# Exponents taken head by head out of PSUM, and batch 1 handled like the later batches

## Chip, cores and metric

One core of a Trainium2 chip runs one program. The metric is the device time of one execution in microseconds, the median of several runs. The core has five engines, named here as in the profile: PE (TensorE), DVE (VectorE), ACT (ScalarE), POOL (GpSimd) and SP (SyncE, which issues all DMAs).

## What is computed

Attention with pooled keys and values (batch 8, 8 heads, 576 queries, head size 64, 72 pooled keys), and a SwiGLU layer on its result (4608 tokens, 512 to 1536 to 512), all in float32 accuracy.

```python
k_p = k.reshape(B, H, Sp, pool, D).mean(axis=3)      # pool = 8, Sp = 72
v_p = v.reshape(B, H, Sp, pool, D).mean(axis=3)
scores = scale * np.matmul(q, k_p.transpose(0, 1, 3, 2))
attn = np.exp(scores - np.max(scores, axis=-1, keepdims=True))
attn = attn / (np.sum(attn, axis=-1, keepdims=True) + 1e-09)
x = np.matmul(attn, v_p)   # then tokens x 512
g = x @ w_gate
out = (g * (1.0 / (1.0 + np.exp(-g))) * (x @ w_val)) @ w_out
```

## The kernel before

The 4608 tokens are cut into nine tiles of 512. Each tile is put together from attention pieces of up to 128 queries of one batch: 40 pieces in all, four in tile 0, five in tile 1 (its first of 64 queries ends batch 0, the other four are of batch 1); the last piece of batch 1 is the first of tile 2. Accurate products are made of halves: an operand is cut into a high and a low float16 part (for the last layer, into an fp32r and a bfloat16 part), and three products replace one.

For each tile and each of 12 chunks of the hidden layer a step makes gate and value products. A plain step (L773 to L777) does 24 products of 512 columns; a fast step (L858, L925) uses Strassen's scheme, with 42 products of 256 columns and some copies by ACT (L937, L939, L946) and additions by DVE (L942, L947) between them. Tiles 0 and 1 are plain. Chunks of weights are loaded and decoded in the first part (L992, `chunk`): shift, sign, join on DVE, ACT and POOL, a sum of sizes over all rows by PE (L303, L304) into one of two attention banks of PSUM, a scale, then high halves by ACT (L384) and low halves by DVE (L389). Later each chunk is converted for fast steps (L789) on DVE, POOL and ACT, and each tile's x is prepared for them (L824). The output layer runs at the end from L1432 on and the change does not touch it.

A piece is asked for (`ask`, L1233) and answered (`answer`, L1243). PE makes scores into two banks, one for even and one for odd heads (L578). DVE takes the maxima of each half out of PSUM (L587) and writes the difference to SBUF (L588), upon which the bank is given back. ACT takes the exponential of all 576 elements in one instruction (L595, L599), DVE sums them by head (L605, L616) and inverts the sums. The batches differ in the rest. `SPLIT = 2` calls batches 0 and 1 old. For an old batch the keys are summed in groups of eight by DVE or POOL (L405 to L407), and the values by PE with a matrix of ones on the diagonal (L501); the weights are normalised (on DVE, or on POOL, L625), cut into halves by ACT and POOL (L638 to L645), turned by a transposing DMA and multiplied with the values so that x comes out turned (L663 to L666), from where ACT and DVE cut it into halves (L689, L693). For a later batch the host has laid out keys and values as six parts, which POOL adds (L1153, `kv_part`, L1169 to L1171) into a place called box, of which there are two by turns; weights are not normalised, the products come out with queries on rows (L673 to L679), DVE divides (L683), ACT and POOL cut into halves (L1332, L1333), and a second transposing DMA turns x (L1337).

The order of all instructions on all engines is made by a planner in the kernel (`Order`, L64): each line of work is a generator that gives, step by step, engine, assumed time and conditions; at each turn the engine with the earliest ready work takes, among the operations that are ready about then, that of the best rank. Banks and buffers are pools that are got and put back (L761). Every engine then works through its queue in that order, and a waiting instruction holds up all behind it.

Of the kernel before, what the change touches and what calls it, by code (L numbers as in the profile page):

```python
# [17 lines left out]
P = 128  # L18
# [6 lines left out]
SPLIT = 2  # L25
# [21 lines left out]
BANKS = "val", "val"  # L47
VALUES = 0.9
LENT = "gate"
PIECE_RANK = 0, 0.5, 1.2, 1.3, 2.2, 2.8, 3.4, 4, 4.6  # L50
# [141 lines left out]
def attention_then_swiglu(  # L192
# [57 lines left out]
    for i in range(4):  # L250
# [16 lines left out]
    logunit = const.tile([P, 1], F32, name="logunit")  # L267
    nc.gpsimd.memset(logunit, LOGUNIT)

    spare = early.tile([P, 2 * NJ * SP + 6 * NJ * P // 2], F32, name="spare", tag="early")  # L270
    ksum = [
        spare[:, i * NJ * SP : (i + 1) * NJ * SP].rearrange("p (j s) -> p j s", j=NJ)
        for i in range(2)
    ]
    vst = spare[:, 2 * NJ * SP :].bitcast(F16).rearrange("p (i j f) -> p i j f", i=6, j=NJ)
    p2s = const.tile([P, B, 4], F32, name="p2s")
    inv = const.tile([P, B, 3], F32, name="inv")
    vst_h, vst_l, vst_f = ([vst[:, 2 * n + i] for i in range(2)] for n in range(3))
# [14 lines left out]
    def fields():  # L293
        for i in range(2):
            nc.gpsimd.memset(halves[i][:, 2 * NJ * P : OLD], 0.0)
            nc.gpsimd.memset(vst_h[i], 0.0)
            nc.gpsimd.memset(vst_l[i], 0.0)
# [138 lines left out]
    KV = H * D + D + NJ * SP  # L436
    TAIL = 2 * SP - P

    def box(b):

        i = b % 2
        if i not in home:
            whole = raw.tile([P, 12 * P * 2], F32, name="box", tag="raw")
# [20 lines left out]
    def move_k(b):  # L464
        nc.scalar.copy(box(b)["k"].rearrange("p j n -> p (j n)"), home["ks", b % 2])

    def move_left(b):
        left = home["left", b % 2]
        nc.scalar.activation(left, left, AF.Copy, scale=inv[:, b, 2:3])

    def spread_left(b):
        left = home["left", b % 2].unsqueeze(1).broadcast_to([P, H, D])
        nc.gpsimd.tensor_mul(box(b)["vm"], left, masks.unsqueeze(2).broadcast_to([P, H, D]))

    def split_v(b, part):
        src, sv = home["vs", b % 2][:, : H * D], inv[:, b, 2:3]
# [104 lines left out]
    def less_max(b, n, pss, sc=None, groups=(0, 1)):  # L581
        sc = sc or buffer(at, [P, H, SP], F32, "sc")
        mx = small.tile([P, 2, GH], F32, name="mx")
        heads = "p (j g) s -> p g j s"
        for g in groups:
            pv = pss[g][:n, : GH * SP].rearrange("p (h s) -> p h s", h=GH)
            nc.vector.tensor_reduce(out=mx[:n, g], in_=pv, axis=AX.X, op=ALU.max)  # L587
            nc.vector.tensor_tensor(  # L588
                out=sc[:n].rearrange(heads, g=2)[:, g], in0=pv,
                in1=mx[:n, g].unsqueeze(2).broadcast_to([n, GH, SP]), op=ALU.subtract,  # L590
            )
        return sc

    def exponentials(n, sc):
        nc.scalar.activation(sc[:n], sc[:n], AF.Exp, scale=EXPSCALE)  # L595

    def weights(b, n, sc):

        nc.scalar.activation(  # L599
            sc[:n], sc[:n], AF.Exp, bias=logunit[:n], scale=EXPSCALE  # L600
        )

    def row_sums(n, sc):
        sm = small.tile([P, H], F32, name="sm")
        nc.vector.tensor_reduce(out=sm[:n], in_=sc[:n], axis=AX.X, op=ALU.add)  # L605
        return sm

    def one_over(n, sm):
        ri = small.tile([P, H], F32, name="ri", bufs=4)
        nc.vector.tensor_scalar_add(sm[:n], sm[:n], 1e-9 * UNIT)  # L610
        nc.vector.reciprocal(ri[:n], sm[:n])
        return ri

    def inverse_sums(n, sc):
        sm = small.tile([P, H], F32, name="sm")
        nc.vector.tensor_reduce(out=sm[:n], in_=sc[:n], axis=AX.X, op=ALU.add)  # L616
        nc.vector.tensor_scalar(
            out=sm[:n], in0=sm[:n], scalar1=1e-9, scalar2=1.0 / UNIT, op0=ALU.add, op1=ALU.mult
        )
        ri = small.tile([P, H], F32, name="ri", bufs=4)  # L620
# [79 lines left out]
    def scales(bs, mt):  # L700
# [10 lines left out]
        for old in (True, False):  # L711
# [5 lines left out]
            if old:  # L717
                nc.vector.tensor_single_scalar(r, r, 1.0 / UNIT, ALU.mult)
# [26 lines left out]

    ahead = [(i, *sub) for i in range(len(tiles)) for sub in tiles[i][2]]
# [10 lines left out]
    def f_room(name):  # L757
# [8 lines left out]
            "x": [(xp, "x1"), (const, "wo0")], "mid": [0, 1, 2], "qt": [0, 1], "xt": [0, 1], "half": [0, 1],  # L766
# [225 lines left out]
    def chunk(c):  # L992
# [23 lines left out]
        if len([w for w in spent if w[0] is raw]) == RAW_USES + 2 and where[0] is raw:  # L1016
            order.done("boxes", t)
# [78 lines left out]
    def pooled_values(b):  # L1096
# [3 lines left out]
        for g in (2, 0, 1):  # L1100
            order.start(("early", (VALUES, SECOND + 0.3)[b] + 0.01 * g), values_in(b, g, where, max(t, tb)))
# [11 lines left out]
        order.start(("early", (VALUES + 0.02, SECOND + 0.32)[b]), left_values(b, t))  # L1113
# [3 lines left out]
        put(BANKS[b], where, max(t, tl[0]))  # L1117
# [36 lines left out]
    def kv_part(b, c, ready):  # L1154
        n, t0 = yield get("mid")
        _, t1 = yield get("load")
# [8 lines left out]
        dst = home["kv", b % 2][:, cs]  # L1165
# [11 lines left out]
    def prep(b):  # L1177

        split = yield flag("boxes")
        if b > SPLIT + 1:  # L1180
            split = yield flag(("split", b - 2))
        box(0)
        box(1)
        t = 0
        for c in range(6):
            order.start(("kv", b + 0.1 * c), kv_part(b, c, split))
# [3 lines left out]
        t = yield op("DVE", 750, lambda: largest(mx, home["vs", b % 2]), t)  # L1190
# [11 lines left out]
        if b - 2 >= SPLIT:  # L1202
# [40 lines left out]
    def answer(t):  # L1243
# [19 lines left out]
        put("qt", t["qt"], tp)  # L1263
        for g in range(2):
# [538 lines left out]
```

## Time and profile before

| | |
|---|---|
| median of 3 runs | 963.73 us (963.48 to 965.11) |
| the profiled execution | 958.7 us |
| its span in the trace | 956.9 us |
| PE busy | 895.9 us (94%) |
| DVE busy | 717.6 us (75%) |
| POOL busy | 580.4 us (61%) |
| ACT busy | 468.9 us (49%) |
| DMA, mean | 153 GB/s |

The page gives busy times of each engine over the span of one execution. A busy PE is not a PE at its peak, since matmuls are pipelined and their ends are modelled. Durations of instructions that follow each other on an engine can overlap, so the distance of two starts is often less than the first one's duration. Where an engine is idle the trace names what ended the wait.

### The profile page before, as it was taken

The numbers are of one execution on the slowest core, as the hardware profiler recorded it, in microseconds if no ns is written. First come the engines' busy times: TensorE is split into PE (matmuls) and PEld (weight loads), VectorE is DVE, ScalarE is ACT, GpSimd is POOL, SyncE is SP. The second block draws the span as 40 slices with busy tenths as digits, with TensorE's granted clock in tenths as the row PEclk, the third lists the DMA queues.
The fourth block names the chain that finished last, engine by engine and source line by source line (L and its number), as shares of the span: only waits on it lengthen the run. The fifth ranks groups of instructions, "written<-read, shape, count | busy, mean of one in ns | idle before, by whom it ended". The sixth has DMA issues, their size and how long they took to land. (4 is left out here: it accounts for less than half of the span.)

```text
span 956.9 us, 17399 instructions
## 1 busy us (share of the span) xinstructions
PE 895.9 (94%) x6636; PEld 629.2 (66%) x6658; DVE 717.6 (75%) x1087; ACT 468.9 (49%) x809; POOL 580.4 (61%) x502
## 2 busy tenths in 40 slices
PE   5788898998989889999999999999899899999998
PEld 5775354444656667888888888888655455555554
DVE  7889898698877798688877645467737769496781
ACT  5578553334245455566664544355624344444442
POOL 3534998989988898454523404022646578678692
PEclk9799899999999999999999999999999999999999
DMA  9947857848748556557572421135560440806301
GB/s 342 289 123 245 264 149 188 227 117 210 187 127 220 171 116 165 151 116 173 136 161 81 97 72 57 56 108 196 195 217 23 164 188 21 309 23 241 111 23 66
DMA packets 134419, 146.53 MB, mean 153 GB/s; under 512 B 81600, under 2 KB 102080, under 8 KB 132032
## 3 DMA queue, kind: packets, MB, share of 16 engines
q1 hardware_dynamic: 134336, 145.42, 51.7%
q8 instruction: 52, 0.85, 0.4%
q14 instruction: 31, 0.25, 0.1%
HBM read 86.51 MB, written 40.89 MB: 133 GB/s over the span
## 5 line engine op out<-in xcount | busy, mean ns | idle before, releaser
L1600 PE MATMUL ps<-low,wsh 128*128 128x512 bf16 x384 | 146.2, 381 | 5.7 <-DVE low L1487 4.1
L879 PEld LDWEIGHTS <-mixed 128*128 128x128 f16 x1332 | 129.2, 98 | 23.4 <-issue 5.6
L879 PEld LDWEIGHTS <-wgv_h 128*128 128x128 f16 x1184 | 114.3, 98 | 33.2 <-issue 15.1
L723 ACT ACTIVATE hf<-ps,un 128x512 f32<-128x512 f32 (+1 forms) x112 | 74.8, 669 | 102.7 <-PE ps L879 62.3
L879 PE MATMUL ps<-xc,mixed 128*128 128x256 f16 x888 | 118.2, 274 | 3.5 <-ACT ps L939 3.5
L726 DVE SCALAR_TENSOR_TENSOR hf<-hf,ps 128x512 f32<-128x512 f32 (+1 forms) x112 | 74.1, 663 | 57.4 <-ACT hf L723 57.0
L879 PE MATMUL ps<-xc,wgv_h 128*128 128x256 f16 x592 | 104.8, 273 | 9.3 <-DVE ps L947 7.7
L777 PE MATMUL ps<-x,wgv_l 128*128 128x512 f16 (+1 forms) x304 | 110.5, 364 | 2.6 <-DVE wgv_l L389 2.6
L775 PE MATMUL ps<-x,wgv_h 128*128 128x512 f16 (+1 forms) x304 | 110.7, 364 | 0.4 <-ACT wgv_h L384 0.4
L776 PE MATMUL ps<-x,wgv_h 128*128 128x512 f16 (+1 forms) x304 | 110.6, 364 | 0.0
L731 DVE SCALAR_TENSOR_TENSOR hf<-ps,un,hf 128x512 f32<-128x512 f32 (+1 forms) x112 | 81.2, 726 | 34.3 <-PE ps L879 27.6
L879 PE MATMUL ps<-x,wgv_h 128*128 128x256 f16 x592 | 103.6, 273 | 2.5 <-ACT rs L937 2.4
L879 PE MATMUL ps<-xc,wgv_l 128*128 128x256 f16 x296 | 80.9, 273 | 0.0
L879 PE MATMUL ps<-x,wgv_l 128*128 128x256 f16 x296 | 80.7, 273 | 0.0
L1487 POOL TENSOR_TENSOR low<-wgv_h,hs 128x1024 bf16<-128x1024 f32 x18 | 51.2, 2867 | 33.2 <-ACT hs L1483 33.2
L1600 PEld LDWEIGHTS <-wsh 128*128 128x128 bf16 x384 | 37.5, 98 | 51.0 <-issue 9.5
L844 POOL TENSOR_TENSOR fx<-fx 128x256 f32<-128x256 f32 x40 | 29.1, 727 | 59.0 <-DVE fx L840 56.6
L879 PEld LDWEIGHTS <-wgv_l 128*128 128x128 f16 x592 | 57.9, 98 | 6.9
L1487 POOL TENSOR_TENSOR low<-wgv_h,more 128x1024 bf16<-128x1024 f32 x16 | 47.2, 2972 | 24.3 <-ACT more L1483 24.3
L879 PE MATMUL ps<-x,mixed 128*128 128x256 f16 x444 | 60.6, 273 | 0.8 <-DVE ps L942 0.8
L1169 POOL TENSOR_TENSOR in<-in 128x576 f32<-128x576 f32 x36 | 55.4, 1540 | 7.8 <-DMA in<-kv_parts 5.7
L1601 PE MATMUL ps<-hs,wsl 128*128 128x512 bf16 x148 | 57.2, 387 | 0.0
(182 smaller groups left out, 2110.0 us busy)
## 6 DMA issues: line engine op xcount, KB each, us to landing
hd<-hf SPq DMA_DIRECT2D x104, 256.0 KB, 2.2
in<-kv_parts SPq DMA_DIRECT2D x36, 576.0 KB, 4.6
ws<-w_all SPq DMA_DIRECT2D x36, 512.0 KB, 5.1
wgv_h<-hd SPq DMA_DIRECT2D x9, 1536.0 KB, 6.7
wgv_l<-hd SPq DMA_DIRECT2D x9, 1536.0 KB, 8.7
out_t<-ob SPq DMA_DIRECT2D x36, 256.0 KB, 2.9
qt<-q_rows SPq DMA_DIRECT2D x32, 256.0 KB, 3.6
wd<-wf SPq DMA_DIRECT2D x12, 256.0 KB, 2.2
```

The costliest lines, as they stand in the source:

```text
L723: nc.scalar.activation(hf, gate, AF.Tanh, scale=un[:, c, 0:1])
L726: nc.vector.scalar_tensor_tensor(out=hf, in0=hf, scalar=1.0, in1=gate, op0=ALU.add, op1=ALU.mult)
L731: nc.vector.scalar_tensor_tensor(out=out, in0=val, scalar=un[:, c, 2:3], in1=hf, op0=ALU.mult, op1=ALU.mult)
L775: nc.tensor.matmul(o, wh, x["h"][:, j, a:e], start=(j == 0), stop=False)
L776: nc.tensor.matmul(o, wh, x["l"][:, j, a:e], start=False, stop=False)
L777: nc.tensor.matmul(o, wl, x["h"][:, j, a:e], start=False, stop=(j == NJ - 1))
L844: t1 = yield op(eng, cost[0], lambda: on.tensor_sub(o, a, b), t1)
L879: nc.tensor.matmul(o, a, b, start=begin and j + n == 0, stop=j == HJ - 1 and n == 2, skip_group_check=True,)
L1169: nc.gpsimd.tensor_add(a[:, :4], a[:, :4], a[:, 4:])
L1487: lambda: on.tensor_sub(low[:, 2 * n : 2 * n + 2], src[:, 2 * n : 2 * n + 2], rows[n].bitcast(F32)),
L1600: nc.tensor.matmul(o, top, where[1][:, c], start=False, stop=False, skip_group_check=True)
L1601: nc.tensor.matmul(o, lo, x_up, start=False, stop=c == HC - 1, skip_group_check=True)
```

## The change

Two things are changed together.

The exponentials. DVE now takes the maxima of both halves (`maxima`), and one DVE instruction on 128x8 elements makes from them a bias per head (`biases`). ACT takes the exponentials head by head straight out of PSUM, eight instructions of 72 elements with the bias as operand, and each also gives its row's sum (`accum_out`). The subtraction and the row sum on DVE are gone. A bank is given back once its four exponentials are done. The inverse of the sums is an addition, for batch 0 also a multiplication, and a reciprocal.

Batch 1. `SPLIT` is 1, so only batch 0 is old. Batch 1's keys and values come as six parts, added by POOL, with a box of its own in the tile `spare` and a buffer of its own for the x that a DMA turns (pool `xt1`). The lines that loaded and pooled its keys and values are gone, PE's summing of its values among them.

Besides: the bank `acc3` is in the pool of value banks from the start; a later batch's preparation (from batch 4 on) begins only when the first piece of the batch ahead of it has been scored (`KV_GATE`); the output weights' chunks are fetched three per tile from tile 4 on (`OUT_FROM`).

```diff
-SPLIT = 2
+SPLIT = 1
-BANKS = "val", "val"
+BANKS = "val"
+OUT_FROM = 4
+KV_GATE = 0
+KV_RANK = 1.4
...
-    def less_max(b, n, pss, sc=None, groups=(0, 1)):
-        sc = sc or buffer(at, [P, H, SP], F32, "sc")
+    def maxima(n, pss):
         mx = small.tile([P, 2, GH], F32, name="mx")
-        heads = "p (j g) s -> p g j s"
-        for g in groups:
+        for g in range(2):
             pv = pss[g][:n, : GH * SP].rearrange("p (h s) -> p h s", h=GH)
             nc.vector.tensor_reduce(out=mx[:n, g], in_=pv, axis=AX.X, op=ALU.max)
-            nc.vector.tensor_tensor(
-                out=sc[:n].rearrange(heads, g=2)[:, g], in0=pv,
-                in1=mx[:n, g].unsqueeze(2).broadcast_to([n, GH, SP]), op=ALU.subtract,
+        return mx
+
+    def biases(b, n, mx):
+        nc.vector.scalar_tensor_tensor(
+            out=mx[:n], in0=mx[:n], scalar=-EXPSCALE, in1=logs[:n, int(b >= SPLIT)], op0=ALU.mult, op1=ALU.add
+        )
+
+    def exponentials(n, pss, mx, sc, sm, g):
+
+        for j in range(NJ):
+            h = 2 * j + g
+            nc.scalar.activation(
+                sc[:n, h], pss[g][:n, j * SP : (j + 1) * SP], AF.Exp, bias=mx[:n, g, j : j + 1], scale=EXPSCALE,
+                accum_out=sm[:n, h : h + 1],
             )
...
+    def one_over(b, n, sm):
         ri = small.tile([P, H], F32, name="ri", bufs=4)
+        nc.vector.tensor_add(sm[:n], sm[:n], tiny[:n, int(b >= SPLIT)])
+        if b < SPLIT:
+            nc.vector.tensor_mul(sm[:n], sm[:n], ones[:n, :H])
         nc.vector.reciprocal(ri[:n], sm[:n])
...
-            "gate": [(ps_gv, "gv0"), acc[0]], "val": [(ps_gv, "gv1")], "wv": [acc[1]], "vs": [acc[2], acc[3]],
+            "gate": [(ps_gv, "gv0"), acc[0]], "val": [(ps_gv, "gv1"), acc[3]], "wv": [acc[1]], "vs": [acc[2]],
...
     def out_weights():
         yield flag("decoded")
         for c in range(NCH):
+            yield flag(("taken", OUT_FROM + c // 3, c % 3 * 4))
...
     def kv_part(b, c, ready):
         n, t0 = yield get("mid")
-        _, t1 = yield get("load")
+        t1 = (yield get("load"))[1] if b > SPLIT else 0
...
     def prep(b):
-        split = yield flag("boxes")
-        if b > SPLIT + 1:
+        split = 0
+        if b > SPLIT:
+            split = yield flag("boxes")
+        if b > SPLIT + 2:
             split = yield flag(("split", b - 2))
-        box(0)
-        box(1)
+            yield flag(("scored", begin[b - 1] + KV_GATE))
+        box(b)
         for c in range(6):
-            order.start(("kv", b + 0.1 * c), kv_part(b, c, split))
+            order.start(("kv", b + 0.1 * c) if b > SPLIT else ("early", KV_RANK + 0.2 * c), kv_part(b, c, split))
...
     def answer(t):
         tp = yield op("PE", 1200 if t["n"] < 12 else 900, lambda: ps.update(scores(b, s0, m, homes)), ta, t0)
+        tp = yield op("DVE", 1200, peaks, tp)
+        sm = small.tile([P, H], F32, name="sm", bufs=4)
         for g in range(2):
-            tm = yield op("DVE", 910, lambda: less_max(b, m, ps, sc, (g,)), tp, ts)
-            put("att", homes[g], tm)
-        tp = tm
+            tp = yield op("ACT", 1300, lambda: exponentials(m, ps, t["mx"], sc, sm, g), tp, ts)
+            put("att", homes[g], tp)
         order.done(("scored", t["n"]), tp)
...
-            n, t0 = yield get("xt")
-            xt = box(n)["xt"][:m]
+            n, t0 = yield get("xt" if b > SPLIT else "xt1")
+            xt = home[n]["xt"][:m]
...
-        for g in range(2):
-            order.start(("early", SECOND + 0.1 * g), keys(1, g))
-        order.start(("early", SECOND + 0.3), pooled_values(1))
...
         for b in range(SPLIT, B):
-            order.start(("prep", b), prep(b))
+            order.start(("prep", b) if b > SPLIT else ("early", KV_RANK + 0.3), prep(b))
```

## Rows read from the trace of the kernel before

**Rows 1.** The page, part 1: busy us, share of span, instructions of each engine.
```profile
PE 895.9 (94%) x6636; PEld 629.2 (66%) x6658; DVE 717.6 (75%) x1087; ACT 468.9 (49%) x809; POOL 580.4 (61%) x502
```

**Rows 2.** Busy time by stretch: stretch, length, busy us of engines, clock, DMA share, GB/s.
```profile
0.00:43.00 43.00, 27.96 (x200) 26.46 (x202) 33.15 (x76) 22.46 (x39) 17.95 (x38) 0.84 0.97 325
43.00:140.00 97.00, 85.18 (x641) 55.28 (x638) 90.40 (x159) 67.50 (x129) 65.06 (x68) 0.95 0.66 197
140.00:400.00 260.00, 240.55 (x1913) 155.60 (x1910) 210.37 (x359) 116.85 (x207) 220.70 (x240) 0.99 0.67 172
400.00:680.00 280.00, 277.82 (x2725) 244.03 (x2723) 196.88 (x376) 147.78 (x301) 92.80 (x96) 1.00 0.44 118
```

**Rows 3.** PE's waits from 43 to 140 us: who waited for whom, total, times, longest.
```profile
PE ps L303 <- DVE sc L588: 5.2, 3, 3.3
PE ps L777 <- DVE wgv_l L389: 2.6, 2, 2.2
PE ps L303 <- DVE p2w L309: 2.0, 3, 0.8
```

**Rows 4.** PE's waits from 140 to 400 us, the longest.
```profile
PE ps L879 <- DVE ps L947: 5.2, 6, 2.0
```

**Rows 5.** Groups of instructions over the span: count, busy us, mean ns, idle before.
```profile
L588 DVE TENSOR_TENSOR sc<-ps,mx 128x288 f32<-128x288 f32 x64 | 29.3, 458 | 6.9 <-POOL box L1333 3.1
L587 DVE TENSOR_REDUCE mx<-ps 128x4 f32<-128x288 f32 x64 | 28.6, 446 | 7.1 <-PE ps L578 7.0
L605 DVE TENSOR_REDUCE sm<-sc 128x8 f32<-128x576 f32 x24 | 17.8, 741 | 0.0
L610 DVE TENSOR_SCALAR sm<-sm 128x8 f32<-128x8 f32 x24 | 8.8, 367 | 0.8
L599 ACT ACTIVATE sc<-sc,logunit 128x576 f32<-128x576 f32 x24 | 18.6, 774 | 23.7 <-DVE sc L588 23.3 <-DVE un L960 0.4
L469 ACT ACTIVATE box<-box,inv 128x64 f32<-128x64 f32 x6 | 2.1, 346 | 3.4 <-DVE inv L312 3.4
L369 ACT ACTIVATION_READ_ACCUMULATOR wgv_h<-mixed 128x1 f32 x24 | 4.5, 190 | 0.0
L1169 POOL TENSOR_TENSOR in<-in 128x576 f32<-128x576 f32 x36 | 55.4, 1540 | 7.8 <-DMA in<-kv_parts 5.7 <-PE ps L578 1.9
L1170 POOL TENSOR_TENSOR in<-in 128x288 f32<-128x288 f32 x36 | 35.4, 984 | 2.8
L1171 POOL TENSOR_TENSOR box<-in 128x144 f32<-128x144 f32 x36 | 23.4, 649 | 2.8
L1333 POOL TENSOR_TENSOR box<-sc,box 128x512 f16<-128x512 f32 x24 | 29.5, 1230 | 23.9 <-ACT box L1332 22.3 <-PE ps L578 1.6
L625 POOL TENSOR_TENSOR sc<-sc,ri 128x576 f32<-128x576 f32 x5 | 7.3, 1455 | 9.0 <-DVE ri L621 8.9
```

**Rows 6.** DVE in order of time: start us, duration us, instruction.
```profile
12.47 0.17 DVE L617 TENSOR_SCALAR sm<-sm 128x8 f32<-128x8 f32 x1
...
38.56 0.74 DVE L693 SCALAR_TENSOR_TENSOR x<-ps,r,x 128x512 f16<-128x512 f32 x1
...
133.78 0.81 DVE L617 TENSOR_SCALAR sm<-sm 128x8 f32<-128x8 f32 x1
```

**Rows 7.** ACT in order of time.
```profile
139.20 0.35 ACT L469 ACTIVATE box<-box,inv 128x64 f32<-128x64 f32 x1 [2.13 <-DVE inv L312]
139.45 0.67 ACT L723 ACTIVATE hf<-ps,un 128x512 f32<-128x512 f32 x1
```

**Rows 8.** PE in order of time, around the first product of tile 0.
```profile
37.56 5.09 PE L501 MATMUL ps<-vr,unit 128*128 128x128 f32 x32
...
43.23 0.28 PE L775 MATMUL ps<-x,wgv_h 128*128 128x256 f16 x1
...
44.22 1.95 PE L501 MATMUL ps<-vr,unit 128*128 128x128 f32 x16
```

**Rows 9.** DMA issues: count, median us from issue to landing.
```profile
x<-box SPq DMA_TRANSPOSE x30, 3.2
```

More of the change, by code (lines that the diff above doesn't have):

```diff
@@ L435, in attention_then_swiglu, with place @@
     home = {}
-    KV = H * D + D + NJ * SP
-    TAIL = 2 * SP - P
+    def place(b):
+        return 2 if b == SPLIT else b % 2
     def box(b):
-        i = b % 2
+        i = place(b)
         if i not in home:
-            whole = raw.tile([P, 12 * P * 2], F32, name="box", tag="raw")
+            if i == 2:
+                whole = spare[:, :BOX]
+            else:
+                whole = raw.tile([P, 12 * P * 2], F32, name="box", tag="raw")
             at16, part = whole.bitcast(F16), {}
@@ L594, in exponentials @@
[L594 to L608, printed above, removed]
-        ri = small.tile([P, H], F32, name="ri", bufs=4)
-        nc.vector.tensor_scalar_add(sm[:n], sm[:n], 1e-9 * UNIT)
-        nc.vector.reciprocal(ri[:n], sm[:n])
-        return ri
@@ L614, in inverse_sums @@
[L614 to L620, printed above, removed]
+        return mx
[3 more added lines that the diff above has]
+        )
@@ L717, in scales @@
             if old:
-                nc.vector.tensor_single_scalar(r, r, 1.0 / UNIT, ALU.mult)
+                nc.vector.tensor_mul(r, r, ones[:, : len(some)])
             ratios |= {b: r[:, n : n + 1] for n, b in enumerate(some)}
@@ L744, in attention_then_swiglu @@
     xs = {}
+    begin = {}
     ahead = [(i, *sub) for i in range(len(tiles)) for sub in tiles[i][2]]
@@ L1016, in chunk @@
         if len([w for w in spent if w[0] is raw]) == RAW_USES + 2 and where[0] is raw:
+            for b in range(2):
+                box(b + 2)
+                put("xt", b, t)
             order.done("boxes", t)
@@ L1100, in pooled_values @@
         for g in (2, 0, 1):
-            order.start(("early", (VALUES, SECOND + 0.3)[b] + 0.01 * g), values_in(b, g, where, max(t, tb)))
+            order.start(("early", VALUES + 0.01 * g), values_in(b, g, where, max(t, tb)))
         t = 0
@@ L1112, in pooled_values @@
         order.done(("scaled", b), t)
-        order.start(("early", (VALUES + 0.02, SECOND + 0.32)[b]), left_values(b, t))
+        order.start(("early", VALUES + 0.02), left_values(b, t))
         t = yield op("ACT", 800, lambda: v_high(b), t)
@@ L1116, in pooled_values @@
         tl = yield flag(("left", b))
-        put(BANKS[b], where, max(t, tl[0]))
+        put(BANKS, where, max(t, tl[0]))
         order.done(("values", b), max(t, tl[1]))
@@ L1164, in kv_part @@
         cs = slice(c * KV // 6, (c + 1) * KV // 6)
-        dst = home["kv", b % 2][:, cs]
+        dst = home["kv", place(b)][:, cs]
         def add():
@@ L1189, in prep @@
         mx = small.tile([P, 1], F32, name="mx1")
-        t = yield op("DVE", 750, lambda: largest(mx, home["vs", b % 2]), t)
+        t = yield op("DVE", 750, lambda: largest(mx, home["vs", place(b)]), t)
         where, t0 = yield get("att")
@@ L1285, in answer @@
         else:
-            te = tp = yield op("ACT", 865, lambda: weights(b, m, sc), tp)
             h, th = yield get("half")
@@ L1717, in all_lines @@
         for n, (i, *sub) in enumerate(ahead):
+            begin.setdefault(sub[1], n)
             t = {"n": n, "at": (i, *sub)}
```

63 lines of the change are left out of this document (32 added, 31 removed).

## The prediction, made before the changed kernel ran

> **What bounds the kernel now.** I read the page's busy times first: TensorE (PE) works 94% of the span [rows 1], so time is PE's work plus PE's gaps, and both can change here. The table of stretches says where the gaps are [rows 2]. PE is idle 15 us in the first 43 us, 11.8 us from 43 to 140 us, 19.5 us from 140 to 400 us and only 2.2 us from 400 to 680 us; behind 680 us the code is untouched. From 43 to 140 us DVE is busy 90.4 of 97 us, PE 85.2, ACT 67.5, POOL 65.1: weights are decoded there on DVE and ACT while tile 0 already consumes them. From 140 to 400 us DVE has 210 and POOL 221 of 260 us, ACT only 117. Then I asked PE's waits. From 43 to 140 us the named ones are mostly DVE's [rows 3]: a weight sum (L303) that can't have an attention bank because DVE has not yet subtracted the maxima out of it (5.2 us), the low halves of decoded weights (2.6 us), scales (2.0 us). From 140 to 400 us the largest is DVE's add inside a fast step, 5.2 us [rows 4]. So before 400 us DVE is the engine that PE waits for, and ACT has room.
>
> **Part 1, exponents by head (all 40 pieces).** Per piece DVE loses two subtractions (458 ns) and the row sum (741 ns) and gains one small combination of maxima and bias. Its nearest row is the addition to the sums on 128x8 elements, 367 ns in the mean [rows 5]; the same kind of instruction lasts 0.17 us when POOL is idle and 0.81 us when it is busy [rows 6]. Net: 0.92 + 0.74 - 0.37 = 1.3 us less DVE per piece (0.85 to 1.5 by the two ends); I take 1.2. ACT loses one exponential of 576 elements (774 ns) and gains eight of 72, each with its sum read out. No row has that shape. The nearest is an activation of 128x64 with a scale tile, 346 ns [rows 5], after which the next one begins 0.25 us later [rows 7]; the read-out lasts 190 ns [rows 5], and may overlap. By starts alone eight take 2.0 us, by durations with read-outs 8 x 0.54 = 4.3 us; I take 2.8, so ACT gains 2.0 us per piece (1.2 to 3.5).
>
> Where this counts: about four pieces are scored before 43 us, six from 43 to 140 us, nineteen from 140 to 400 us, eleven later. From 43 to 140 us DVE falls by 6 x 1.2 = 7.2 us to 83, ACT rises by 12 to 80 of 97: both below PE's 85. Of the 9.8 us of PE waits named for DVE in that stretch [rows 3] I credit 4 us (8 at most, since DVE is not the only one late; a loss of 3 if ACT now ends the chain). From 140 to 400 us DVE falls by 19 x 1.2 = 23 us and ACT goes to 155 of 260; I credit 4 of PE's 19.5 us idle (8 at most; a loss of 3 where ACT's copies inside a fast step stand behind four exponentials). The spreading of the later batches' key and value loads (each batch's begin with the first scores of the batch ahead of it) and of the output weights (three chunks per tile from tile 4) goes the same way, since POOL's 221 of 260 us carry these additions beside the conversion of weights; it is inside this credit. From 400 to 680 us PE has 2.2 us of gaps, and 11 x 2.0 = 22 us more on ACT, from 148 of 280: +1 us, 0 to +6.
>
> **Part 2, batch 1 as the later ones.** PE loses the pooling of batch 1's values: 32 records in 5.09 us right ahead of tile 0's first product, and 16 more in 1.95 us a little later [rows 8]. The first product stands behind them in PE's queue, at 43.23 us. What would be late next is the x of piece 1, a DVE operation that begins at 38.56 us and takes 0.74 us [rows 6]. So at most 3.9 us come back at the start. But two pieces must come through the longer ACT chain first, with 2 x 2.0 us more of ACT, part of it hidden in ACT's 20.5 us idle before 43 us [rows 2]. I take -2 (from -3.9 to +2). The later 16 records lie inside the busy stretch; I take -1 (0 to -1.95).
>
> POOL's new work before 140 us: six parts of 1540 + 984 + 649 ns = 3.17 us [rows 5], in place of the two key sums that had the same three shapes, so four parts net, 12.7 us; five subtractions for x (1230 ns) come, five normalisations (1455 ns) go. Net some +11.5 us on 65 [rows 2, 5]. It has room, but it stands beside DVE's decoding. By the shapes in the code DMA gets 3.5 MB in place of 2.75 MB, 0.8 MB more, 2.4 us at the stretch's 325 GB/s [rows 2] before 43 us; it delays chunk loads that wait for DVE anyway, and costs if DVE is no longer late. I count it inside the bounds of the start.
>
> The x of batch 1's pieces now goes through a POOL subtraction of 1230 ns [rows 5] and a transposing DMA of 3.2 us to landing [rows 9], with one buffer, and each transpose stands in SP's queue ahead of loads, where the chunk loads and the part loads wait behind it. DVE's and ACT's shares are alike in the old and the new way, so a piece's x comes 1.23 + 3.2 = 4.4 us later. It is paid once, where tile 1 waits for its last piece, and only if tile 0's products don't cover it: +1 us (0 to +4.4).
>
> **Sum.** -2 - 1 - 4 + 1 - 4 + 1 = -9 us. The profiled execution took 958.7 us with a span of 956.9; it becomes 949.7. The median of the runs is 963.73 us, 5.0 above that execution, and I let this distance stand: 954.7 us, and 949 to 960 for this case by half of each bound.
>
> **Rivals.**
> *A wait for ACT takes the place of the wait for DVE, and is longer (slower).* Today a bank of scores comes free after a reduction and a subtraction, 446 + 458 ns of DVE per half [rows 5]. Afterwards it needs both reductions, the bias and four exponentials: 0.9 + 0.3 + 1.4 = 2.6 us for the first half, 4 for the second, so some 2 us later. The weight sums need such a bank, and they stand in PE's queue ahead of the tile's products. Three of them waited 5.2 us between 43 and 140 us [rows 3]. If seven sums of the early stage wait 2 us each, that is 14 us: 954.7 + 14 = 968.7 us. It decides as soon as the exponentials begin more than some 2 us late behind decoding on ACT. Against it: ACT's 67.5 of 97 us, and the order is planned anew with these holds in it. Chance 0.25.
>
> *POOL's additions take back what DVE won (no change).* The 128x8 instruction shows 0.17 against 0.81 us with POOL idle or busy [rows 6]. If each of the 11.5 us more of POOL stopped DVE, the 4 us credited from 43 to 140 us and the 3 us at the start would go, and two more behind them: 963 to 964 us. For it: the new parts are added just where DVE decodes. Against it: the two removed DVE operations are replaced by so little that 0.64 us of lock per piece still leaves 0.85 us. Chance 0.13. The Trainium skill says this as a rule (SBUF — State Buffer, section Who interferes with whom): a DVE instruction with two SBUF inputs, or in a 2-port mode, and a GpSimd instruction exclude each other for the whole instruction, the second blocks fully. The rows' 0.17 and 0.81 us agree with that. By the rule the removed subtractions, which read PSUM and one SBUF operand, and the row sum never met POOL, while the new bias combination does; it would leave less of the credit than I count.
>
> *PE becomes the only bound (much faster).* The start gives 3.9 us, the rest of the pooling 1.95 and the two stretches 8 each, less the 1 + 1 us for the handover and the late ACT: -19.9 us, 943.8 us. For it: PE's gaps before 400 us are 46 us in all [rows 2]. Against it: DVE, ACT and PE all come to 80 to 85 of 97 us in one chain, so none can be hidden wholly. Chance 0.15.
>
> **How the numbers follow.** Forecast 0.47, much faster 0.15, no change 0.13, slower 0.25. About 0.2%, 1.9 us, is what a measurement of this kernel can tell from no change. Faster: 0.47 + 0.15 = 0.62; within 0.2%: 0.13; slower: 0.25. The range goes from the fast case's centre to the slow one's, 944 to 969 us, and leaves out about half of either, 0.07 and 0.11.
>
> **What would show it.** Right: PE's first product of tile 0 begins at 40 to 42 us; DVE falls by some 45 us over the span and ACT's eight exponentials take 2.6 to 3 us from first start to next; PE's idle time from 43 to 140 us falls to about 8 us and the last decoded chunk comes 5 us or more earlier; POOL's L1169 rows begin before 40 us. Wrong: weight sums that wait for exponentials for over 5 us in all, a gap of PE between tile 0 and tile 1 behind a transposing DMA, or fast steps that wait for ACT's copies after 400 us.

## The result, and the profile after

| | changed kernel | kernel before, same chip | ratio, 95% interval |
|---|---|---|---|
| first set | 950.62 us (949.98 to 951.39, 4 runs) | 963.61 us (4 runs) | 0.9872 [0.9842, 0.9901] |
| second set | 954.01 us (951.32 to 955.95, 4 runs) | 962.45 us (7 runs) | 0.9915 [0.9887, 0.9942] |
| third set | 954.13 us (950.28 to 954.91, 6 runs) | 961.92 us (17 runs) | 0.9905 [0.9883, 0.9927] |

The change makes the kernel faster by 8 to 13 us; the sum of the prediction was 9. The 14 runs of the changed kernel lie between 949.98 and 955.95 us, 6 us apart, so a difference below 2 or 3 us between two kernels settles nothing. "The changed kernel" without a set means the first set's profiled execution: 950.87 us with a span of 948.8 us, 8.1 less than before's.

First the busy times of the changed kernel's page, to be held against [rows 1]:

```profile
PE 887.7 (94%) x6687; PEld 628.9 (66%) x6687; DVE 666.6 (70%) x1016; ACT 539.4 (57%) x1408; POOL 584.0 (62%) x516
```

Then its table of stretches (length; busy time and count of PE, PEld, DVE, ACT, POOL; granted PE clock; DMA share; GB/s), against [rows 2]:

```profile
0.00:43.00 43.00, 20.76 (x140) 19.37 (x141) 32.04 (x69) 30.21 (x87) 24.15 (x44) 0.86 0.99 332
43.00:140.00 97.00, 87.45 (x661) 56.86 (x661) 86.29 (x153) 75.80 (x216) 75.17 (x79) 0.92 0.80 212
140.00:400.00 260.00, 248.86 (x2134) 174.67 (x2135) 186.80 (x335) 151.09 (x507) 192.10 (x223) 0.99 0.59 148
400.00:680.00 280.00, 271.06 (x2617) 236.45 (x2615) 180.60 (x350) 175.92 (x477) 116.16 (x114) 0.99 0.52 145
```

PE's busy time falls by 8.2 us (895.9 to 887.7) and the span by 8.1: PE's idle time as a whole stays at 61 us. By stretch it moved. From 140 to 400 us it falls from 19.5 to 11.1 us (14.9 and 13.7 in the other two sets), from 43 to 140 us from 11.8 to 9.6 (7.4, 9.0). But before 43 us it grows from 15.0 to 22.2, and from 400 to 680 us from 2.2 to 8.9 (7.4, 7.7). The stretches are cut at fixed times, so they don't hold quite the same work in the two kernels. DVE is down by 51 us, ACT up by 70.

What PE waits for in these stretches (total, times, longest, us), against [rows 3, 4]; the first two rows lie before 43 us, the next two from 43 to 140, the next five from 140 to 400, the last two from 400 to 680:

```profile
PE ps L587 <- DVE p2w L314: 4.6, 1, 4.6
PE ps L587 <- ACT sc L606: 4.4, 2, 3.9
...
PE ps L668 <- ACT sc L606: 3.6, 1, 3.6
PE ps L587 <- ACT sc L606: 1.8, 1, 1.8
...
PE ps L875 <- DVE hf L726: 3.1, 3, 2.3
PE ps L875 <- DVE ps L943: 2.9, 4, 1.2
PE ps L587 <- ACT sc L606: 2.5, 2, 1.8
PE ps L668 <- ACT sc L606: 1.7, 2, 1.1
PE ps L771 <- DMA x<-spare: 1.4, 1, 1.4
...
PE ps L875 <- DVE ps L943: 4.4, 6, 1.4
PE ps L875 <- DVE ps L938: 3.2, 2, 2.6
```

The weight sums no longer wait for DVE's subtraction [rows 3]. In its place scores (L587) and value products (L668) wait for exponentials (L606), which hold the banks that they need: 4.4 us before 43 us, 5.4 from 43 to 140 us, 4.2 from 140 to 400 us.

The new operations, as groups (count, busy us, mean ns):

```profile
L606 ACT ACTIVATE sc<-ps,mx 128x72 f32<-128x72 f32 x256 | 78.5, 334 | 18.8 <-DVE mx L598 16.0 <-DVE un L956 1.5 <-DVE sm L613 1.2
...
L606 ACT ACTIVATION_READ_ACCUMULATOR sc<-ps,mx 128x1 f32 x256 | 56.4, 220 | 0.0
...
L598 DVE SCALAR_TENSOR_TENSOR mx<-mx,logs 128x8 f32<-128x8 f32 x32 | 16.2, 507 | 1.2
...
L613 DVE TENSOR_TENSOR sm<-sm,tiny 128x8 f32<-128x8 f32 x32 | 11.5, 358 | 5.7 <-ACT sc L606 5.7
```

Five marks, each the start of an instruction (a gate operation is DVE's L721, L726 before):

| us | before | changed |
|---|---|---|
| PE's first product of tile 0 | 43.2 | 48.4 |
| last low half of a decoded chunk | 137.3 | 128.1 |
| DVE's last gate operation of tile 0 | 141.4 | 133.6 |
| the same of tile 3 | 381.2 | 358.0 |
| the same of tile 8 | 685.5 | 675.4 |

So the changed kernel starts tile 0 5 us later, has decoded 9 us earlier, leads by 23 us after tile 3 and by 10 after tile 8. Four plain steps became fast ones: 304 matmuls at L775 before, 272 at L771 now, eight for a step.

### The profile page after: what moved, and what is told of

Read it like the earlier page. It is cut to its first block, busy times and chain, and to the rows that moved or that the text cites. A ratio compares the mean times of both kernels' runs of the same rounds, so it can differ in the third digit from the quotient of the medians.

```text
span 948.8 us, 17997 instructions
## 1 busy us (share of the span) xinstructions
PE 887.7 (94%) x6687; PEld 628.9 (66%) x6687; DVE 666.6 (70%) x1016; ACT 539.4 (57%) x1408; POOL 584.0 (62%) x516
## 5 line engine op out<-in xcount | busy, mean ns | idle before, releaser
L875 PEld LDWEIGHTS <-mixed 128*128 128x128 f16 x1404 | 136.4, 98 | 24.9 <-issue 5.5
L875 PEld LDWEIGHTS <-wgv_h 128*128 128x128 f16 x1248 | 121.0, 98 | 32.5 <-issue 14.3
L875 PE MATMUL ps<-xc,mixed 128*128 128x256 f16 x936 | 123.2, 274 | 1.0 <-ACT ps L935 0.9
L721 DVE SCALAR_TENSOR_TENSOR hf<-hf,ps 128x512 f32<-128x512 f32 (+1 forms) x112 | 74.3, 664 | 63.0 <-ACT hf L718 62.6
L606 ACT ACTIVATE sc<-ps,mx 128x72 f32<-128x72 f32 (+1 forms) x320 | 97.8, 330 | 22.2 <-DVE mx L598 19.4
L875 PE MATMUL ps<-x,wgv_h 128*128 128x256 f16 x624 | 109.2, 273 | 0.0
L726 DVE SCALAR_TENSOR_TENSOR hf<-ps,un,hf 128x512 f32<-128x512 f32 (+1 forms) x112 | 81.6, 729 | 37.8 <-PE ps L875 26.8
L771 PE MATMUL ps<-x,wgv_h 128*128 128x512 f16 (+1 forms) x272 | 98.3, 361 | 1.4 <-DMA x<-spare 1.4
L772 PE MATMUL ps<-x,wgv_h 128*128 128x512 f16 (+1 forms) x272 | 98.0, 360 | 0.5 <-DVE x L688 0.4
L773 PE MATMUL ps<-x,wgv_l 128*128 128x512 f16 (+1 forms) x272 | 97.8, 360 | 0.4 <-DVE wgv_l L394 0.3
L649 POOL TENSOR_TENSOR half<-sc,half 128x448 f16<-128x448 f32 (+1 forms) x35 | 39.6, 1130 | 57.2 <-ACT half L644 51.2
L1169 POOL TENSOR_TENSOR in<-in 128x576 f32<-128x576 f32 x42 | 62.3, 1483 | 13.8 <-DMA in<-kv_parts 13.8
L606 ACT ACTIVATION_READ_ACCUMULATOR sc<-ps,mx 128x1 f32 (+1 forms) x320 | 69.4, 217 | 0.0
```

The lines of the kernel that those rows point to most:

```text
L606: nc.scalar.activation(sc[:n, h], pss[g][:n, j * SP : (j + 1) * SP], AF.Exp, bias=mx[:n, g, j : j + 1], scale=EXPSCALE, accum_out=sm[:n, h ...
L721: nc.vector.scalar_tensor_tensor(out=hf, in0=hf, scalar=1.0, in1=gate, op0=ALU.add, op1=ALU.mult)
L726: nc.vector.scalar_tensor_tensor(out=out, in0=val, scalar=un[:, c, 2:3], in1=hf, op0=ALU.mult, op1=ALU.mult)
L771: nc.tensor.matmul(o, wh, x["h"][:, j, a:e], start=(j == 0), stop=False)
L772: nc.tensor.matmul(o, wh, x["l"][:, j, a:e], start=False, stop=False)
L773: nc.tensor.matmul(o, wl, x["h"][:, j, a:e], start=False, stop=(j == NJ - 1))
```

## Experiments

### Each part alone

The kernel before with part 1 alone (batch 1 stays old), planned anew:

```diff
...
-            tm = yield op("DVE", 910, lambda: less_max(b, m, ps, sc, (g,)), tp, ts)
-            put("att", homes[g], tm)
+            tp = yield op("ACT", 1300, lambda: exponentials(m, ps, t["mx"], sc, sm, g), tp, ts)
+            put("att", homes[g], tp)
...
```

> The kernel before with the exponentials by head alone; batch 1 stays old, the order of work is planned anew. If the gain came from DVE's relief in the decoding stretch, the last low half of a decoded chunk begins before 134 us (137.3 before, 128.1 after), tile 0's first product stays 1 to 5 us later than the 43.2 us of before, and the time is 955 to 959 us. If the gain came from batch 1's values leaving PE (7 us of matmuls), this kernel shows nothing of it: 961 to 965 us.

Measured: 953.47 us, before 960.58, ratio 0.9915 [0.9890, 0.9941]. The last low half begins at 131.5 us, the first product at 47.2. Faster by 7 us, a little more than the theory of DVE's relief said, and it comes out of PE's gaps: PE is busy 3.0 us more than before (898.9) and idle 7.7 us less (53.3). But tile 0's last gate operation comes no earlier (141.7 us, 141.4 before); the lead appears by tile 3 (370.1 against 381.2).

The changed kernel without part 1 (old exponentials; batch 1, its box and the spread loads as changed), planned anew:

```diff
...
-            tp = yield op("ACT", 1300, lambda: exponentials(m, ps, t["mx"], sc, sm, g), tp, ts)
-            put("att", homes[g], tp)
+            tm = yield op("DVE", 910, lambda: less_max(b, m, ps, sc, (g,)), tp, ts)
+            put("att", homes[g], tm)
...
```

> The changed kernel with the old way of exponentials (two subtractions and a row sum on DVE, one exponential of 576 elements on ACT); batch 1, the boxes and the spread loads as changed, planned anew. If DVE's relief brought the gain, the last low half begins at 136 us or later, tile 0's first product at 43 us or earlier, and the time is 958 to 963 us. If PE's removed matmuls brought it, PE's busy time is 7 us under before's and the time is 951 to 955 us.

Measured: 954.10 us, ratio 0.9927 [0.9902, 0.9952]. Last low half at 139.6, first product at 43.2 (before: 43.2), PE busy 887.9 us. So the marks are those of the first theory and the time is that of its rival: this half, with the spread loads in it, brings 6.5 us by itself, without any relief of DVE. Here the gain is PE's work: 8.0 us less busy, 3.0 us more idle (64.0). The first product doesn't come earlier although the 32 rows of pooling ahead of it [rows 8] are gone. It needs the x of piece 1, and DVE's operation for that, which began at 38.56 us before [rows 6], now begins at 44.61; PE's second product waits for it (start, duration, idle time ahead of it):

```profile
44.61 0.74 DVE L699 SCALAR_TENSOR_TENSOR x<-ps,r,x 128x512 f16<-128x512 f32 x1
...
45.40 0.37 PE L783 MATMUL ps<-x,wgv_h 128*128 128x256 f16 x1 [1.79 <-DVE x L699]
```

7.1 and 6.5 make 13.6, both together bring 8 to 13. Beside the changed kernel this one is only 0 to 3.5 us slower, with 49 us more of DVE's work and 66 us less of ACT's.

### DVE's work put back

The changed kernel in its own order, with the removed DVE work done into scratch:

```diff
             biases(b, m, t["mx"])
+            for g in range(2):
+                nc.vector.tensor_tensor(out=junk..., in0=ps[g]..., in1=t["mx"]..., op=ALU.subtract)
...
         def ratios():
+            nc.vector.tensor_reduce(out=again[:m], in_=sc[:m], axis=AX.X, op=ALU.add)
             t["ri"] = one_over(b, m, sm)
```

> The changed kernel in its own order, with the DVE work that was taken out put back as work that nobody reads: two subtractions from PSUM and one row sum per piece, 1.2 us. If DVE paces the decoding, the last low half goes back to 136 to 139 us (128.1 in the changed kernel) and the time to 956 to 962 us. If PE's own removed work is the gain and DVE had room, 950 to 953 us. DVE's busy time must rise by about 45 us.

Measured: 969.72 us (967.75 to 971.51), ratio to before 1.0085 [1.0054, 1.0116]. The busy times of its page:

```profile
PE 893.3 (92%) x6665; PEld 632.7 (65%) x6687; DVE 719.1 (74%) x1136; ACT 539.6 (56%) x1408; POOL 583.0 (60%) x516
```

Two of its stretches:

```profile
43.00:140.00 97.00, 87.51 (x635) 57.68 (x633) 89.86 (x170) 75.63 (x210) 71.44 (x74) 0.87 0.70 200
140.00:400.00 260.00, 240.96 (x2004) 165.56 (x2005) 203.21 (x372) 143.16 (x490) 189.90 (x219) 0.98 0.56 146
```

And the largest of PE's waits from 140 to 400 us:

```profile
PE ps L876 <- DVE ps L944: 10.4, 9, 2.8
```

DVE is up by 52 us on the changed kernel, and the time by 16 (third set) to 19 us (first set), more than I expected. Last low half 135.4. The kernel is behind the changed one by 7.0 us after tile 0, by 13.6 after tile 3, by 17.3 after tile 4 and by the same 17 after tile 8: all of the price is paid before about 440 us. From 43 to 140 us PE's idle time is that of the changed kernel (9.5 us against 9.6), but its granted clock is 0.87 against 0.92 (0.89, 0.92 in the other sets) and it does fewer matmuls; from 140 to 400 us its idle time is 19.0 us against 11.1 (14.9, 13.7), and the wait for DVE's add inside fast steps (L944, L943 in the changed kernel) 10.4 us against 2.9 (5.1 in the third set). This is the price in an order that was planned without that work. The kernel without part 1, above, does that work in an order planned for it, without ACT's new work, and is slower than the changed kernel by 3.5 us at most.

### ACT's work lightened

The changed kernel in its own order, with two exponentials of 288 elements per piece in place of eight of 72. Four heads share one head's bias, and the row sums are a constant: that part of the computation is changed.

```diff
-        for j in range(NJ):
-            nc.scalar.activation(sc[:n, h], pss[g][...], AF.Exp, bias=mx[:n, g, j : j + 1], ..., accum_out=...)
+        nc.scalar.activation(sc[:n]..., pv, AF.Exp, bias=mx[:n, g, 0:1], scale=EXPSCALE)
```

> The changed kernel in its own order, but ACT takes two exponentials of 288 elements per piece in place of eight of 72, with one head's bias for four heads, and the row sums are a constant, so weights and divisors are not the reference's. ACT loses some 1.5 us per piece. If the exponentials cause the late start and the waits of fast steps, tile 0's first product begins at 45 to 46 us (48.35), PE's idle time from 400 to 680 us is under 5 us (8.9), and the time is 944 to 948 us. If ACT's work is hidden, 949 to 951 us.

Measured: 945.68 us (943.76 to 946.89), ratio 0.9829 [0.9799, 0.9858]. One of its stretches, ACT being the fourth engine:

```profile
400.00:680.00 280.00, 271.57 (x2623) 236.33 (x2622) 185.19 (x351) 157.01 (x314) 119.72 (x114) 1.00 0.53 150
```

ACT's 62 us less (539.4 to 477.3) are worth 5 to 8 us, so ACT's longer work does cost. The first product moves from 48.4 to 46.8 only, and PE's gaps from 400 to 680 us stay at 8.4 us (8.9): those are not the exponentials', against what I expected.

### The start: the table, POOL's additions, PE's place

ACT loads its table at 10.37 us, behind the wait for the first bias; before, it did so at 0.71 us, with nothing behind it. From ACT's timeline in the changed kernel: start, duration, engine, line and operation:

```profile
10.37 1.28 ACT L606 ACT_TABLE_LOAD   x1 [10.37 <-DVE mx L598]
11.67 0.32 ACT L606 ACTIVATE sc<-ps,mx 128x72 f32<-128x72 f32 x1
11.89 0.19 ACT L606 ACTIVATION_READ_ACCUMULATOR sc<-ps,mx 128x1 f32 x1
11.98 0.31 ACT L606 ACTIVATE sc<-ps,mx 128x72 f32<-128x72 f32 x1
```

```diff
     nc.gpsimd.tensor_add(warm[:, 1:2], warm[:, 0:1], warm[:, 0:1])
+    nc.scalar.activation(warm[:, 1:2], warm[:, 0:1], AF.Exp)
```

> The changed kernel in its own order with one activation on a column of zeros at the start, so that ACT's table is loaded while ACT is idle and not behind the wait for the first bias (1.28 us at 10.37 us). If the late start is a chain from there, tile 0's first product begins 1 to 1.3 us earlier (48.35), and the time falls by 0.5 to 1.3 us to 949.3 to 950.1. If the start is covered by the decoding, the first product moves and the time stays at 950.6.

Measured: 951.42 us (948.21 to 953.20), ratio 0.9886 [0.9857, 0.9915]; ACT's table load begins at 0.71 us again, and the first product at 47.0, 1.4 us earlier. The changed kernel again, beside it:

> The changed kernel itself, beside the other runs of this call on the same chip: 950.6 us again, within 1.5 us, so that differences of 2 us between kernels with the same order can be read.

Measured: 954.01 us, so it didn't come again within 1.5 us. The intervals overlap; 2.6 us between the two are a hint and no more.

POOL's work for batch 1 shortened (its keys and values are then sums of two in place of eight):

```diff
         def add():
             a = part["in"]
-            nc.gpsimd.tensor_add(a[:, :4], a[:, :4], a[:, 4:])
-            nc.gpsimd.tensor_add(a[:, :2], a[:, :2], a[:, 2:4])
+            if b > SPLIT:
+                ...
             nc.gpsimd.tensor_add(dst, a[:, 0], a[:, 1])
```

> The changed kernel in its own order, but POOL leaves out the first two of the three additions for each of batch 1's six parts (1540 + 984 ns, 15.1 us in all before 140 us), so batch 1's keys and values are sums of two in place of eight. If POOL's additions hold DVE up while it decodes, the bias combination's mean falls below 0.45 us (0.51), the last low half begins 1.5 us or more earlier (128.1) and the time is 946 to 949 us. If they are hidden, less than 0.5 us: 950 to 951.

Measured: 950.00 us (948.82 to 950.58), ratio 0.9875 [0.9849, 0.9900]: 4 us under the changed kernel of the same set, level with that of the first. The bias combination's mean is 500 ns (508 beside it), the last low half 128.4 (130.5 beside it, 128.1 in the first set). Of the two signs I had named for a lock the first is not there; the second is there beside the changed kernel of the same set (2.1 us earlier) and not beside that of the first. POOL's additions cost 0 to 4 us; which, stays open.

PE's work ahead of the first product put back, as 32 float32 matmuls that nobody reads:

```diff
         wh, wl = wgv_h[:, c, i, j, :], wgv_l[:, c, i, j, :]
+        if "filled" not in x_home:
+            x_home["filled"] = True
+            for _ in range(32):
+                nc.tensor.matmul(o[:, :P], unit, unit, start=True, stop=True)
```

> The changed kernel in its own order with 32 float32 matmuls of 128x128, the number and shape that pooled batch 1's values, put back as work that nobody reads right ahead of tile 0's first product (they took 5.09 us at the slow clock and would take 4 to 5 here). If PE's place ahead of the first product is the path, the end comes 4 to 5 us later: 955 to 958 us. If the decoding behind it sets the pace, the end of tile 0 (133.6 us) and the time move by less than 1.5 us: 950 to 953.

PE's timeline around it (start, duration):

```profile
48.65 8.99 PE L774 MATMUL ps<-unit 128*128 128x128 f32 x64
57.48 0.27 PE L775 MATMUL ps<-x,wgv_h 128*128 128x256 f16 x1
```

They took 8.8 us: a float32 matmul stands in the trace as two rows, so 32 of them are twice the 32 rows that went. Measured: 955.19 us (954.83 to 958.07), ratio 0.9931 [0.9911, 0.9952]. Beside it in the third set:

> The changed kernel, as the measure for the others of this call: its medians so far are 950.6 and 954.0 us, so 950 to 954, with differences between executions of the same program of some 3 us.

Measured: 954.13 us. So 8.8 us of PE work right ahead of tile 0 make tile 0 end 6.9 us later (142.2 against 135.3), the median 1.1 us and the profiled execution 3.3 us longer. Neither case fits: tile 0 does move, and the end less. The lag is 5.0 us after tile 4 and 2.2 after tile 5. Of these 2.8 us, 1.8 are one wait of PE for a DVE add, 2.55 us in the changed kernel of this set and 0.78 here:

```profile
448.16 1.44 PE L875 MATMUL ps<-x,mixed 128*128 128x256 f16 x6 [2.55 <-DVE ps L938]
...
451.68 0.82 PE L879 MATMUL ps<-x,mixed 128*128 128x256 f16 x6 [0.78 <-DVE ps L942]
```

That add stands behind a turned x (shown below), so part of the lag is made up where PE would have waited for a DMA. Where the rest went is not shown.

### The spread loads taken back

The changed kernel without the two holds, planned anew:

```diff
         for c in range(NCH):
-            yield flag(("taken", OUT_FROM + c // 3, c % 3 * 4))
             n, t0 = yield get("mid")
...
             split = yield flag(("split", b - 2))
-            yield flag(("scored", begin[b - 1] + KV_GATE))
```

> The changed kernel without the two holds that spread loads: the output weights are fetched as soon as decoding ends, and a later batch's parts as soon as its box is free; the order is planned anew. If the spreading caused PE's gaps from 400 to 680 us (8.9 us against 2.2 of before), these fall under 5 us and the gaps from 140 to 400 us rise above 14 us (11.1); the time is 950 to 955 us. If the gaps at 400 us and later belong to the exponentials on ACT, they stay at 8 to 10 us.

Measured: 963.01 us (957.11 to 965.13, 12 runs), ratio to before 1.0000 [0.9981, 1.0020]. The whole gain is gone, against the 950 to 955 us that I expected. Two of its stretches:

```profile
140.00:400.00 260.00, 239.87 (x1936) 157.58 (x1936) 188.99 (x329) 153.66 (x499) 208.99 (x234) 0.98 0.69 179
400.00:680.00 280.00, 274.29 (x2676) 240.10 (x2674) 179.94 (x340) 161.91 (x472) 94.97 (x103) 0.99 0.39 114
```

PE's waits from 140 to 400 us:

```profile
PE ps L587 <- ACT sc L606: 5.2, 4, 2.1
PE ps L771 <- DMA x<-spare: 4.8, 1, 4.8
PE ps L668 <- ACT sc L606: 4.7, 1, 4.7
```

As expected the gaps move: 20.1 us from 140 to 400 us (11.1), 5.7 from 400 to 680 (8.9). The loads move 179 GB/s in place of 148 before 400 us, POOL has 17 us more to do there, and PE waits 4.8 us for a turned x and 9.9 us for exponentials. The four plain steps return (304 matmuls at L771). The loss lies in tile 1: its last gate operation comes 97.5 us after tile 0's (135.6 to 233.1), in the changed kernel 87.2 (133.6 to 220.8). Part 1 alone has no holds either and is 7 us faster than before; this kernel differs from it by batch 1's new way (with the bank `acc3`) and gains nothing. So, in these orders, batch 1's new way without the holds costs what part 1 brings, and the holds win it back. Since the order is planned anew each time, up to some 5 us of such a difference may be the order's (below).

### Less DVE work still

The sum of exponentials is at least one in float32, so the added 1e-9 doesn't change it. Early table, and without the addition, in the changed kernel's own order:

```diff
-        nc.vector.tensor_add(sm[:n], sm[:n], tiny[:n, int(b >= SPLIT)])
```

> The changed kernel in its own order with the early table and without the addition of 1e-9 to the sums, which a float32 sum of at least one doesn't feel: one DVE instruction of 358 ns in the mean less per piece, 14.3 us over the span. By the loaded kernel's slope (46 us of DVE more cost 17 us) that gives 5 us: 944 to 947 us, last low half about 2 us earlier (128.1). If DVE has become uncritical, the time is that of the early table alone, 949 to 950.6.

Measured: 947.15 us (945.33 to 948.32), ratio 0.9844 [0.9820, 0.9868]: 6.9 us under the changed kernel beside it and 4.3 under the one with the early table alone. It beats both kernels. The loaded kernel's slope, 17 us for 52 of DVE, gives 4.7 for these 14.3, in the same order as there. The last low half hardly moves (127.9 against 128.5 with the early table): the place I had named was wrong, the lead over the early table alone comes in tile 2 (1.8 us) and tile 5 (2.8 us).

The same, planned anew with measured lengths (1180 ns for four exponentials, 250 ns for the inverse sums):

```diff
...
-            tp = yield op("ACT", 1300, lambda: exponentials(m, ps, t["mx"], sc, sm, g), tp, ts)
+            tp = yield op("ACT", 1180, lambda: exponentials(m, ps, t["mx"], sc, sm, g), tp, ts)
...
```

> The kernel with the early table and without the addition of 1e-9, planned anew with the measured lengths: 1180 ns for four exponentials (1300 assumed) and 250 ns for the inverse sums (450). The planner's own end moves by 1 us. If the removed DVE work is what counts and the order little, 945 to 949 us; if the order of the changed kernel was a lucky one, 950 to 955 us.

Measured: 952.27 us (949.05 to 952.87), ratio 0.9885 [0.9862, 0.9907]. The same work in another order costs 5 us: first product at 51.8, last low half at 136.2. Differences of up to 5 us between kernels that were planned anew can be the order's alone.

## Why the prediction was right, and where its steps were not

The time was right, by terms that were mis-sized on both sides, and so in part by luck. For the profiled execution the sum said 949.7 us and 950.87 were measured; the medians are 950.6, 954.0 and 954.1 where it had 954.7. The 5.0 us that I added for the median belong to before's profiled execution alone: that of the changed kernel lies 0.3 to 1.9 us above its median in all three sets. The split was not met: of the -9 us I gave -3 to PE's work (start and later pooling) and -6 to its gaps. In the profiled pair PE's work is 8.2 us less and its gaps are as long as before.

**The start (-2) had the wrong sign.** The first product came 5.1 us later. The step that failed: I took the x of piece 1 to be ready where it had been, its DVE operation at 38.56 us [rows 6], so that 3.9 us came free once the pooling ahead of the product was gone. In the new orders that x is itself late: the operation begins at 44.61 us with batch 1's part alone, at 44.40 with part 1 alone and at 48.34 in the changed kernel, and tile 0's products, all but the very first, come behind it. With the new exponentials PE waits 4.4 us for them, because the scores of the next piece need the bank, and 4.6 us for a scale (L314) that comes late in DVE's queue, DVE being busy 11.8 of 13 us from 30 to 43 us. What delays x with the old ones is not traced further. I had ACT's 20.5 idle us before 43 us [rows 2] hide part of the longer chain. Some 9 of these lay before 10 us, when nothing is scored yet; from there to 43 us ACT is now busy 30.2 of 33 us, and the table is loaded in that time too (1.4 us of the first product, by the early table). Nor was the start worth its length: 8.8 us of PE there cost 1 us by the medians and 3 by the profiled executions.

**Decoding (-4) had the right mechanism.** PE's gaps from 43 to 140 us went to 9.6, 7.4 and 9.0 us where I had said 8, and the last low half came 9.2 us earlier (5 or more foreseen). With part 1 alone it came 5.8 earlier, without it 2.3 later. That the earlier decoding is what shortens the run is not shown: with part 1 alone tile 0 ended no earlier.

**What a microsecond of DVE is worth was the term most out of size.** I credited 8 us for 48 us of DVE in the pieces. In the changed order, 52 us put back cost 16 to 19 us; with the order planned for it, DVE's old work in exchange for ACT's new costs 0 to 3.5 us. Against it stands ACT: I took +1 us and a lost start for its longer work; 62 us less of it, also in a fixed order, are worth 5 to 8 us. The two together make an estimate of some 5 to 12 us for DVE's old work in an order planned for it: the high price holds for an order that doesn't know of the work. The eight exponentials themselves cost less than I took: they start every 0.29 to 0.30 us, 2.35 us for eight (2.8 taken). Too small a gain and too small a price cancelled.

**140 to 400 us (-4) was about in the range (8 at most), for another reason.** The gaps fell by 4.5 to 8.3 us. I called the spreading of the loads a part of DVE's credit. Without it the run is as long as before, and PE waits there for exponentials and for a turned x. So the holds are a term of their own, of up to 9 us, of which the order may have some; they make up for batch 1's new way, as part 1 alone gains 7 us without them.

**400 to 680 us (+1) came to +5.2 to +6.8, by a path I had not named.** I feared copies behind exponentials. With the exponentials lightened the gaps stay; they shrink without the holds, which push loads into this stretch. One gap of it, in the timeline of the changed kernel (start, duration, idle time ahead of it and what ended it):

```profile
435.67 1.61 SPq L1340 DMA_TRANSPOSE x<-box  x1
...
438.16 0.44 SPq L1161 DMA_DIRECT2D in<-kv_parts  x1
...
441.41 1.23 DVE L836 TENSOR_TENSOR fx<-x 128x1024 f32<-128x1024 f16 x1 [3.74 <-DMA x<-box]
...
442.55 0.43 DVE L938 TENSOR_TENSOR ps<-ps,rs 128x256 f32<-128x256 f32 x1
...
443.03 0.27 PE L875 MATMUL ps<-x,mixed 128*128 128x256 f16 x1 [2.63 <-DVE ps L938]
```

SP issues the transpose of x at 435.67 us, and it lands at 441.3 us, with batch parts issued meanwhile. DVE waits 3.74 us for the next tile's x, which that DMA turns; the add of a fast step (L938) stands behind it on DVE, and PE waits 2.63 us for that add. The path of the other gaps in this stretch is not traced. Another part of the lost lead is no loss. In tiles 4 and 5 PE has more to do. Of the kernel before, by stretch from mark to mark:

```profile
381.20:446.90 65.70, 64.66 (x648) 56.19 (x647) 51.44 (x101) 41.72 (x81) 33.35 (x39) 1.00 0.59 142
446.90:512.50 65.60, 65.60 (x683) 57.07 (x682) 49.89 (x103) 37.65 (x73) 23.79 (x27) 1.00 0.62 146
```

Of the changed kernel:

```profile
358.00:428.40 70.40, 66.47 (x675) 55.55 (x674) 50.88 (x96) 45.74 (x149) 48.06 (x55) 1.00 0.70 177
428.40:499.20 70.80, 68.15 (x698) 58.74 (x696) 46.72 (x99) 48.33 (x152) 41.02 (x46) 0.98 0.72 175
```

Before, PE is busy 130.3 of 131.3 us; now 134.6 of 141.2. Eleven pieces are scored there (176 score matmuls at L587) where it was nine (144 at L578). So of the 10 us given back, 4.4 are work that came later and 5.5 are gaps.

**Batch 1's turned x (+1)** cost PE 1.4 us at L771 (1.3 in the third set): right.

**Value pooling later (-1) and PE's work.** All of the pooling is 7.0 us of PE [rows 8]. Four plain steps (24 products of 512 columns) that became fast (42 of 256) save 4 x 6 x 0.108 us (from start to start of 256 columns) = 2.6 more, which I had not foreseen. PE's busy time falls by 8.2, 4.3 and 6.4 us in the three sets; it moves with the granted clock too. How much of it is time by itself is not shown: the filler's 8.8 us ahead of tile 0 raised PE's busy time by 4.6 us and the span by 3.3 (third set).

**The rivals.** *A wait for ACT in place of DVE's* is real, as one term and not as the outcome: scores and products wait for exponentials for 4.4, 5.4 and 4.2 us in the three stretches before 400 us. The weight sums, of which it spoke, don't wait for them in any stretch. The loaded kernel's 969.7 us lie near its 968.7 by chance: there it is DVE's add that PE waits for. *POOL takes back DVE's gain*: the bias combination took 507 ns in the mean where I took 367, still a small part of the 1.66 us that went; DVE fell by 51 us (45 foreseen). How much of POOL's additions is time, the shortened ones don't settle. *PE the only bound* fell: its idle time is still 61 us.

## What to carry to other kernels

Before you credit a gap to the instruction that stands ahead of it in a queue, ask what the next instruction needs, and whether that is still ready as early in the new order: here the x that was there at 39 us came 6 us later once the pooling was gone. Cost an edit of a chain by what each engine gives and takes, with a kernel for each direction in the same order, and again planned anew: a load put back shows its price in that one order (16 to 19 us here), while DVE's old work in place of ACT's new, planned for, cost 0 to 3.5 us. When loads are moved to a later stage, look which queue there will stand behind a DMA.

## What the runs showed of the hardware

**A small DVE instruction can wait through several of POOL's.** Around 376 us in the changed kernel (start, duration):

```profile
375.71 1.03 POOL L649 TENSOR_TENSOR half<-sc,half 64x448 f16<-64x448 f32 x1
...
375.97 2.55 DVE L598 SCALAR_TENSOR_TENSOR mx<-mx,logs 128x8 f32<-128x8 f32 x1
...
376.70 0.42 POOL L650 TENSOR_TENSOR half<-sc,half 64x128 f16<-64x128 f32 x1
...
377.09 1.40 POOL L1169 TENSOR_TENSOR in<-in 128x576 f32<-128x576 f32 x1
...
379.51 0.27 PE L875 MATMUL ps<-xc,wgv_h 128*128 128x256 f16 x1 [1.05 <-DVE sm L613]
379.51 0.32 ACT L606 ACTIVATE sc<-ps,mx 128x72 f32<-128x72 f32 x1
```

The bias combination is listed from 375.97 to 378.52 us, 2.55 us, where it takes 0.16 to 0.17 with POOL idle; it ends as POOL's third instruction in a row ends (377.09 + 1.40 = 378.49). PE is idle 1.05 us for a DVE operation that stands behind it in DVE's queue. Not every one waits: ten of the 40 lasted 0.17 us or less with POOL busy all the while. The Trainium skill (SBUF — State Buffer, section Who interferes with whom) has the two engines exclude each other for a whole instruction; the row agrees, and the wait is longer than one instruction: here three went by.

**Late clock at the start.** In the changed kernel PE, busy only 5.9 of 13 us from 30 to 43 us, is granted 0.67 from 43 to 55 us, a mean of its two levels; before, busy 11.1 of 13, it has 1.00 there. Before:

```profile
30.00:43.00 13.00, 11.12 (x92) 10.51 (x93) 11.28 (x22) 7.30 (x15) 7.76 (x12) 0.60 0.85 311
43.00:55.00 12.00, 10.66 (x119) 9.59 (x116) 11.63 (x19) 9.70 (x17) 4.57 (x5) 1.00 0.76 177
```

Changed:

```profile
30.00:43.00 13.00, 5.89 (x43) 5.27 (x43) 11.82 (x28) 11.09 (x22) 9.92 (x13) 0.63 0.95 336
43.00:55.00 12.00, 10.45 (x91) 9.13 (x91) 11.76 (x19) 9.90 (x32) 11.35 (x9) 0.67 0.72 219
```

**The read-out of an accumulator costs less than it is listed at.** Listed at 220 ns in the mean, it is followed by the next exponential after 0.09 us, from its own start at 11.89 to 11.98 us in the timeline above.
